# Strided attention heads: from one fused VectorE instruction per query row and key row to GpSimd products summed by VectorE

## The chip, the core and the metric

The program runs on one core of a Trainium2 chip. The metric is the device time of one execution in microseconds (us). A core has five engines that run side by side, each through its own queue in order: PE (TensorE, matrix products into PSUM), DVE (VectorE), ACT (ScalarE), POOL (GpSimd) and SP (SyncE, which issues the DMAs here). An instruction that waits for a semaphore holds everything behind it on its engine.

## The reference

Attention over 8 batches, 8 heads, 576 positions and 64 channels, followed by a feed-forward block on 4608 tokens of width 512 and inner width 2048, all in float32:

```python
scores = scale * np.matmul(q, k.transpose(0, 1, 3, 2))
mask_local = (rel >= 0) & (rel < stride)                     # stride = 32
mask_strided = (rel >= 0) & (pos[None, :] % stride == pos[:, None] % stride)
masks = np.stack([mask_local if h < H // 2 else mask_strided for h in range(H)], axis=0)
scores = np.where(masks[None, :, :, :], scores, -1000000000.0)
attn = softmax(scores)                                       # over the keys
x = attn @ v, as (tokens, heads * channels)
h = x @ w_in
out = (0.5 * h * (1.0 + erf(h * inv_sqrt2))) @ w_out
```

Heads 0 to 3 are local: a query sees the 32 positions up to its own. Heads 4 to 7 are strided: a query at position 32 r + p sees only positions 32 c + p with c up to r, that is at most 18 keys.

## The kernel before, in words

**Feed-forward.** The 4608 tokens are cut into 12 tiles of 384, the inner width into 16 blocks of 128, which makes 192 steps n. A step has an H product (`ffn_h`, L619 to L621: 12 matmuls of 384 columns), a Gelu in place on ACT (L628), a split of the result into a rounded high part `gh` (ACT, L630) and the remainder `gl` (DVE, L632), and an O product (`ffn_o`, L658 to L660: 9 matmuls of 512 columns, accumulated over the 16 blocks). The split, for weights and for the tokens `xh` and `xl` too, gives float32 precision out of TensorE's shorter format. H has two PSUM banks, so H of step n+2 may begin only when `gl` of step n has read the bank of step n. After the first 16 steps the program emits steps in pairs (`pair`, L867): H(n), H(n+1), O(n-2), O(n-1). The pools `gh` and `gl` have three buffers each.

**Local heads.** Their scores are matmuls (L297), their softmax is DVE and ACT work (L311, L315, L318 to L321), and their products with the values are matmuls (L337). In the main loop each token tile has a *visit*, once in 16 steps, in which PE does the value products of one tile and the scores of the next.

**Strided heads.** The 32 residues p times 4 heads make the 128 partitions. `sq`, `sk`, `sv` hold queries, keys and values as [128 partitions, 18 rows, 64 channels]. The first 12 rows of batch 0 are done by matmuls in the opening (L387 to L441). All other rows are cut into units of up to four query rows (`PLACE`, 37 units u from 3 to 39). For a unit, `strided_qk` (L480) takes the product of one query row with one key row by one DVE instruction that multiplies 64 channels and sums them (L494), 1290 times in all; each such instruction is followed in the profile by a read of the accumulator into `sc`. Then DVE takes the maximum and subtracts it (L502, L503), ACT takes the exponential (L504), DVE sums and divides (L520 to L524), and `strided_av` (L508) adds probability times value row to `acc`, one DVE instruction of 64 channels for each pair of rows (L534 for the first, L536 for the rest). DVE transposes `acc` into `xs` (L544); ACT and DVE split that into `xh` and `xl` (`to_x`, L235).

**What sets the order.** In the opening a list, `START`, sets the order of jobs on DVE, ACT, PE and SP: `c` splits the weights, `f` is a feed-forward step of the first tile, `u1` a part of the strided units of tile 1 (`unit_job`, L580). In the main loop (L889) only ACT and PE keep the program's order; DVE and POOL instructions are placed by the framework's scheduler. `run_strided` (L688) hands out the list `strided` in portions set by the costs that stand beside each operation (0.137 for a query-key product, 0.196 for a probability-value product, and so on), so that the work of a tile is spread over the steps before that tile is due. POOL's queue holds the masks and fills of the opening and one fill of `sc` for each unit (L487).

Of the kernel before, what the change touches and what calls it, by code (L numbers as in the profile page):

```python
# [10 lines left out]
F32 = mybir.dt.float32  # L11
# [50 lines left out]
HIGH_V = [0, 1, 2, 3, 5, 6, 10, 13]  # L62
QUOT_V = (0, 1)
ROWS = [(vi, b, r) for vi, (b, r0, r1) in enumerate(VISITS) for r in range(r0, r1)]


def units(most):
# [15 lines left out]
def attn_ffn_kernel(ctx: ExitStack, tc: tile.TileContext, qk, vl, qka, va, qs, ks, vs, w, out):  # L83
# [118 lines left out]
                lpool.tile([P, DM], F32, name=f"PT_{name}", tag="PT", bufs=2))  # L202

    def small(name):
        return [lpool.tile([P, 4], F32, name=f"{k}_{name}", tag=k, bufs=4) for k in ("nm", "ss", "rs")]

    def softmax_parts(blocks, nq, scores, msk, p, nmax, ssum, rs, dve):

# [271 lines left out]
    def strided_qk(u):  # L480
        vi, _, r0, nr, t, k = PLACE[u]
        W = r0 + nr
        ops = []

        def init():
            s = spool.tile([P, UR, NR], F32, name=f"sc_{u}", tag="sc", bufs=3)[:, 0:nr]
            nc.gpsimd.memset(s[:, :, 0:W], NEG)  # L487
            ss[u] = s
        ops.append((0.0, init))
        for c in range(W):  # L490
            for r in range(max(0, c - r0), nr):
                def f(r=r, c=c):
                    junk = spool.tile([P, D], F32, name=f"junk_{u}_{r}_{c}", tag="junk", bufs=4)
                    nc.vector.tensor_tensor_reduce(  # L494
                        junk, sq[vi, "q"][:, r0 + r, :], sq[vi, "k"][:, c, :], 1.0, 0.0,
                        ALU.mult, ALU.add, ss[u][:, r, c:c + 1])
                ops.append((0.137, f))

        def sm():
            s = ss[u][:, :, 0:W]  # L500
            m = spool.tile([P, UR], F32, name=f"m_{u}", tag="m")[:, 0:nr]
            nc.vector.tensor_reduce(m, s, AX.X, ALU.max)  # L502
            nc.vector.tensor_tensor(s, s, m.unsqueeze(2).to_broadcast([P, nr, W]), ALU.subtract)  # L503
            exps.append((u, lambda: nc.scalar.activation(s, s, AF.Exp, scale=SC)))  # L504
        ops.append((0.25, sm))
        return ops

    def strided_av(u):  # L508
# [13 lines left out]
        def quotients():  # L522
            s = ss[u][:, :, 0:W]
            nc.vector.tensor_tensor(s, s, every(z, W), ALU.mult)  # L524
            ss[u, "acc"] = spool.tile([P, UR, D], F32, name=f"acc_{u}", tag="acc", bufs=3)[:, 0:nr]
        ops += [(0.1, zsum), (0.1, lambda: nc.vector.tensor_scalar_add(z, z, 1e-9)),
                (0.1, lambda: nc.vector.reciprocal(z, z)), (0.1, quotients)]
        for c in range(W):
            for r in range(max(0, c - r0), nr):
                def f(r=r, c=c):  # L530
                    acc = ss[u, "acc"]
                    wgt = ss[u][:, r, c:c + 1]
                    if c == 0:
                        nc.vector.tensor_scalar_mul(acc[:, r, :], sq[vi, "v"][:, c, :], wgt)  # L534
                    else:
                        nc.vector.scalar_tensor_tensor(  # L536
                            acc[:, r, :], sq[vi, "v"][:, c, :], wgt, acc[:, r, :], ALU.mult, ALU.add)
                ops.append((0.196, f))

        def fin():  # L540
            acc = ss.pop((u, "acc"))
# [13 lines left out]
    def alternate(us, what, first):  # L555


        todo = []
        for u in us:
            ops = what(u)  # L560
            todo.append([[x] for x in ops[:first]] + [ops[first:-1]] + [[ops[-1]]])
        res = []
        for ops in zip(*todo):
            if len(ops[0]) == 1:
                res += [x[0] for x in ops]
                continue
            rows_ = []
            for u, x in zip(us, ops):
                r0, nr = PLACE[u][2:4]
                key = [r for c in range(r0 + nr) for r in range(max(0, c - r0), nr)]  # L570
                rows_ += [[f for k, f in zip(key, x) if k == r] for r in range(nr)]
            used = [-9] * len(rows_)
            while any(rows_):
                k = max((k for k in range(len(rows_)) if rows_[k]),
                        key=lambda k: (min(len(res) - used[k], 3), len(rows_[k])))
                used[k] = len(res)
                res.append(rows_[k].pop(0))
        return res

    def unit_job(us):  # L580

        n = 8
        qk = alternate(us, strided_qk, 1)
        for _, f in qk[:len(us)]:
            f()
        for i in range(len(us), len(qk), n):
            for _, f in qk[i:i + n]:
                f()
            yield
        for e in [x for x in exps if x[0] in us]:  # L590
# [1 line left out]
            e[1]()  # L592
        yield
        av = alternate(us, strided_av, 4)
        for i in range(0, len(av), n):
            for _, f in av[i:i + n]:
                f()
            yield
        todo = [x for x in splits if x[2] in us]
# [24 lines left out]
    def ffn_g(n):  # L624
        hp = hps.pop(n)
        gh = gpool.tile([P, TT], F32R, name=f"gh_{n}", tag="gh")
        gl = gpool.tile([P, TT], F32R, name=f"gl_{n}", tag="gl")
        nc.scalar.activation(hp, hp, AF.Gelu)  # L628
        yield
        nc.scalar.copy(gh, hp)  # L630
        yield
        nc.vector.tensor_tensor(gl, hp, gh.bitcast(F32), ALU.subtract)  # L632
        gs[n] = (gh, gl)
# [325 lines left out]
```

## Time and profile before

| What | us |
|---|---|
| time, median of 2 runs (875.14 to 876.11) | 875.62 |
| span of the profiled execution | 875.6 |
| PE busy | 853.6 |
| DVE busy | 707.1 |
| ACT busy | 490.3 |
| POOL busy | 17.6 |

The span of the profiled execution lies between the two timed runs, so that a sum made against it can be read as a time without a correction. The profile lists groups of instructions as line, engine, operation, output and inputs with their shapes and count, then busy time with the mean duration of one, then the idle time of the engine just before them and what ended it. Busy time of an engine counts overlapping instructions once; the busy time of a group adds up durations, so that groups of short DVE instructions, which overlap by a part of their length, add up to more than DVE's busy time.

### The profile page before, as it was taken

To read this page: it belongs to the slowest core of one execution; us is meant where nothing else is said; L and a number is where in the kernel's file an instruction comes from. 1 tells how busy PE (TensorE), PEld (TensorE's weight loads), DVE (VectorE), ACT (ScalarE), POOL (GpSimd) and SP (SyncE) were. 2 spreads that over 40 slices of the span, in tenths; PEclk is the share of its full clock that TensorE was granted. 3 is DMA by queue.
4 is the path that set the end of the run, shared out by engine and by line. 5 is a ranking of instruction groups with operands and counts; after the bars stand their busy time and mean duration, and the time that the engine had idled before them with its cause. 6 is when DMAs were issued, how large, how long until landed. Compare 5 with 4: busy or idle time off the path is not lost.

```text
span 875.6 us, 19724 instructions
## 1 busy us (share of the span) xinstructions
PE 853.6 (97%) x6082; PEld 768.4 (88%) x6082; DVE 707.1 (81%) x4901; ACT 490.3 (56%) x1005; POOL 17.6 (2%) x89
## 2 busy tenths in 40 slices
PE   6999999999999999999999999999999999999998
PEld 5787898899898989899889899999988988898997
DVE  6988999889989998998999879799898896751111
ACT  6978586466456274368366466546545735733222
POOL 5000100000000000000000000000000000000000
PEclk9799999999999999999999999999999999999999
DMA  9695211320310221310302221131032011000001
GB/s 350 226 372 207 96 42 24 123 76 7 128 45 19 93 75 33 98 49 8 110 28 67 67 67 43 34 123 46 8 101 79 9 34 44 32 8 6 31 1 37
DMA packets 34553, 66.68 MB, mean 76 GB/s; under 512 B 6800, under 2 KB 16528, under 8 KB 34448
## 3 DMA queue, kind: packets, MB, share of 16 engines
q1 hardware_dynamic: 34448, 65.43, 22.0%
q8 instruction: 48, 0.79, 0.4%
q14 instruction: 57, 0.47, 0.2%
HBM read 51.64 MB, written 9.44 MB: 70 GB/s over the span
## 4 chain that ended last, share of the span: by engine, by line
PE 69%; DVE 17%; DMA 5%; ACT 5%; issue 2%; SPq 2%; DVEq 0%; ACTq 0%
PE H L619 11%; PE O L659 11%; PE O L660 11%; PE H L621 11%; PE O L658 11%; PE H L620 11%; DVE acc L536 5%; DVE junk L494 4%; DMA ws<-in_w_dram 3%; DVE gl L632 2%; ACT L504 1%; SPq L326 1%; PE X_L L337 1%; ACT PT_L L315 1%; DVE xl L238 1%
## 5 line engine op out<-in xcount | busy, mean ns | idle before, releaser
L619 PE MATMUL H<-xh,w 128*128 128x384 f32 x768 | 260.8, 340 | 5.6 <-DVE gl L632 5.4
L620 PE MATMUL H<-xl,w 128*128 128x384 f32 x768 | 258.6, 337 | 0.8 <-DVE xl L238 0.8
L621 PE MATMUL H<-xh,w 128*128 128x384 f32 x768 | 258.9, 337 | 0.0
L628 ACT ACTIVATE H<-H 128x384 f32<-128x384 f32 x192 | 91.4, 476 | 287.4 <-PE H L621 230.5
L536 DVE SCALAR_TENSOR_TENSOR acc<-sv,sc,acc 128x64 f32<-128x64 f32 x1158 | 248.8, 277 | 0.6
L660 PE MATMUL O<-w,gl 128*128 128x512 f32 x576 | 226.8, 394 | 0.1
L659 PE MATMUL O<-w,gh 128*128 128x512 f32 x576 | 226.2, 393 | 0.0
L658 PE MATMUL O<-w,gh 128*128 128x512 f32 x576 | 225.0, 391 | 0.5 <-ACT gh L630 0.5
L494 DVE CUSTOM_DVE_ANT_0 junk<-sq,sk 128x64 f32<-128x64 f32 x1290 | 204.5, 217 | 3.3 <-DMA sk<-in_ks_dram 3.1
L632 DVE TENSOR_TENSOR gl<-H,gh 128x384 fp32r<-128x384 f32 x192 | 105.9, 551 | 105.8 <-ACT gh L630 105.7
L619 PEld LDWEIGHTS H<-xh,w 128*128 128x128 f32 x768 | 144.9, 189 | 12.7 <-DVE gl L632 7.5
L620 PEld LDWEIGHTS H<-xl,w 128*128 128x128 f32 x768 | 144.9, 189 | 4.8 <-DVE xl L238 1.2
L621 PEld LDWEIGHTS H<-xh,w 128*128 128x128 f32 x768 | 144.9, 189 | 0.1
L630 ACT CAST gh<-H 128x384 fp32r<-128x384 f32 x192 | 92.3, 481 | 69.2 <-PE O L659 62.8
L660 PEld LDWEIGHTS O<-w,gl 128*128 128x128 f32 x576 | 108.3, 188 | 24.4 <-DVE gl L632 1.6
L658 PEld LDWEIGHTS O<-w,gh 128*128 128x128 f32 x576 | 108.5, 188 | 21.1 <-ACT gh L630 1.0
L659 PEld LDWEIGHTS O<-w,gh 128*128 128x128 f32 x576 | 108.4, 188 | 20.6
L494 DVE DVE_READ_ACCUMULATOR2_ANT sc<- 128x1 f32 x1290 | 103.7, 80 | 0.0
L628 ACT ACT_TABLE_LOAD x62 | 79.5, 1283 | 1.1
L504 ACT ACT_TABLE_LOAD x35 | 44.9, 1283 | 0.6
L315 ACT ACTIVATE PT_L<-P_L,nm_L 128x64 f32<-128x64 f32 x132 | 44.3, 339 | 0.3
L315 ACT ACT_TABLE_LOAD x26 | 33.4, 1283 | 0.5
(114 smaller groups left out, 493.0 us busy)
## 6 DMA issues: line engine op xcount, KB each, us to landing
ws<-in_w_dram SPq DMA_DIRECT2D x16, 1023.8 KB, 9.9
qk<-in_qk_dram SPq DMA_DIRECT2D x36, 320.0 KB, 5.1
out_dram<-ob SPq DMA_DIRECT2D x34, 256.0 KB, 2.1
vl<-in_vl_dram SPq DMA_DIRECT2D x36, 192.0 KB, 3.9
sk<-in_ks_dram SPq DMA_DIRECT2D x8, 576.0 KB, 4.7
sv<-in_vs_dram SPq DMA_DIRECT2D x8, 576.0 KB, 4.0
band<-PT_L SPq DMA_DIRECT2D x240, 16.0 KB, 1.8
sq<-in_qs_dram SPq DMA_DIRECT2D x4, 576.0 KB, 4.8
```

The source lines that it names most:

```text
L315: nc.scalar.activation(pv[:, :, h, :], p1[:, h * 2 * QB:(h + 1) * 2 * QB].rearrange("p (c t) -> p c t", c=2), AF.Exp, bias=nm[:, h:h + 1], ...
L494: nc.vector.tensor_tensor_reduce(junk, sq[vi, "q"][:, r0 + r, :], sq[vi, "k"][:, c, :], 1.0, 0.0, ALU.mult, ALU.add, ss[u][:, r, c:c + 1])
L536: nc.vector.scalar_tensor_tensor(acc[:, r, :], sq[vi, "v"][:, c, :], wgt, acc[:, r, :], ALU.mult, ALU.add)
L619: nc.tensor.matmul(hp, w1[f][:, 0, c, :], xh[:, c, :], start=(c == 0), stop=False)
L620: nc.tensor.matmul(hp, w1[f][:, 0, c, :], xl[:, c, :], start=False, stop=False)
L621: nc.tensor.matmul(hp, w1[f][:, 1, c, :], xh[:, c, :], start=False, stop=(c == NC - 1))
L628: nc.scalar.activation(hp, hp, AF.Gelu)
L630: nc.scalar.copy(gh, hp)
L632: nc.vector.tensor_tensor(gl, hp, gh.bitcast(F32), ALU.subtract)
L658: nc.tensor.matmul(o, gh[:, sl], w2[f][:, 0, :], start=(f == 0), stop=False)
L659: nc.tensor.matmul(o, gh[:, sl], w2[f][:, 1, :], start=False, stop=False)
L660: nc.tensor.matmul(o, gl[:, sl], w2[f][:, 0, :], start=False, stop=(f == NF - 1))
```

## The change

The 1290 query-key instructions and the 1290 probability-value instructions are replaced. For one query row, GpSimd multiplies the row with up to nine key rows at once (up to 576 elements in a partition) into a buffer, and one VectorE reduction sums each run of 64 channels into `sc`. For the values GpSimd multiplies the value rows, read with the channel outside and the key row inside (a step of 64 elements), with the probabilities of the query row, and VectorE sums over the key rows into `acc`. Longer rows are cut into equal pieces. The buffers are two (`NPROD`), so that a product is emitted ahead of the sum of the piece before it. The products carry no cost in the list `strided`, the sums carry 0.15 + elements / 960. `small` has three buffers in place of four, `acc` two in place of three, and `gl` two in place of three. `alternate` no longer interleaves the rows of the units; `unit_job` yields five portions for queries and keys and six for the values.

```diff
+PRODUCT = 576
+NPROD = 2
+def MULT(nc):
+    return nc.gpsimd
+def cuts(n, most):
+    k = -(-n // most)
+    at = [i * n // k for i in range(k + 1)]
+    return list(zip(at, at[1:]))
+def staged(pieces, size, product, sums):
+    ops, late = [], []
+    for x in pieces:
+        c = 0.15 + size(*x) / 960
+        ops.append((0.0 * c, lambda x=x: product(*x)))
+        late.append((c, lambda x=x: sums(*x)))
+        if len(late) == NPROD:
+            ops.append(late.pop(0))
+    return ops + late
...
-        return [lpool.tile([P, 4], F32, name=f"{k}_{name}", tag=k, bufs=4) for k in ("nm", "ss", "rs")]
+        return [lpool.tile([P, 4], F32, name=f"{k}_{name}", tag=k, bufs=3) for k in ("nm", "ss", "rs")]
...
-                    nc.vector.tensor_tensor_reduce(
-                        junk, sq[vi, "q"][:, r0 + r, :], sq[vi, "k"][:, c, :], 1.0, 0.0,
-                        ALU.mult, ALU.add, ss[u][:, r, c:c + 1])
-                ops.append((0.137, f))
+        def product(r, lo, hi):
+            n = hi - lo
+            prods[r, lo] = pr = spool.tile([P, PRODUCT], F32, name=f"pq_{u}_{r}_{lo}", tag="prod", bufs=NPROD)[
+                :, 0:n * D].rearrange("p (c d) -> p c d", c=n)
+            MULT(nc).tensor_tensor(pr, sq[vi, "q"][:, r0 + r, :].unsqueeze(1).to_broadcast([P, n, D]),
+                                   sq[vi, "k"][:, lo:hi, :], ALU.mult)
+        def sums(r, lo, hi):
+            nc.vector.tensor_reduce(ss[u][:, r, lo:hi], prods.pop((r, lo)), AX.X, ALU.add)
...
-            ss[u, "acc"] = spool.tile([P, UR, D], F32, name=f"acc_{u}", tag="acc", bufs=3)[:, 0:nr]
+            ss[u, "acc"] = spool.tile([P, UR, D], F32, name=f"acc_{u}", tag="acc", bufs=2)[:, 0:nr]
...
-                        nc.vector.tensor_scalar_mul(acc[:, r, :], sq[vi, "v"][:, c, :], wgt)
-                    else:
-                        nc.vector.scalar_tensor_tensor(
-                            acc[:, r, :], sq[vi, "v"][:, c, :], wgt, acc[:, r, :], ALU.mult, ALU.add)
-                ops.append((0.196, f))
+        def product(r, lo, hi):
+            n, w_ = hi - lo, r0 + r + 1
+            prods[r, lo] = pr = spool.tile([P, PRODUCT], F32, name=f"pv_{u}_{r}_{lo}", tag="prod", bufs=NPROD)[
+                :, 0:n * w_].rearrange("p (d c) -> p d c", d=n)
+            MULT(nc).tensor_tensor(pr, sq[vi, "v"][:, 0:w_, lo:hi].rearrange("p c d -> p d c"),
+                                   ss[u][:, r, 0:w_].unsqueeze(1).to_broadcast([P, n, w_]), ALU.mult)
+        def sums(r, lo, hi):
+            nc.vector.tensor_reduce(ss[u, "acc"][:, r, lo:hi], prods.pop((r, lo)), AX.X, ALU.add)
...
-        gl = gpool.tile([P, TT], F32R, name=f"gl_{n}", tag="gl")
+        gl = gpool.tile([P, TT], F32R, name=f"gl_{n}", tag="gl", bufs=2)
```

DVE's queue in the main loop, before, from the remainder `gl` of step 64 on (the number behind a name is its step, unit or row; `ISA` is the fused product and sum, with the read of its accumulator behind it):

```order
L632 TENSOR_TENSOR gl_64_4806<-H_64_4792,gh_64_4805 128x384
L238 TENSOR_TENSOR xl_5_4811<-xs_16_4682,xh_5_4810 128x2x128
L536 SCALAR_TENSOR_TENSOR acc_17_4847<-sv_6_4416,sc_17_4418,acc_17_4847 128x64
L544 STREAM_TRANSPOSE xs_17_4951<-acc_17_4847 128x256
L494 ISA junk_20_0_0_5330,sc_20_5328<-sq_6_4012,sk_6_4014 128x64
L494 ISA sc_20_5328 128x1
L494 ISA junk_20_1_0_5332,sc_20_5328<-sq_6_4012,sk_6_4014 128x64
L494 ISA sc_20_5328 128x1
```

And now, from the same step to the remainder of the step behind it and a little further:

```order
L654 TENSOR_TENSOR gl_64_3976<-H_64_3962,gh_64_3975 128x384
L265 TENSOR_TENSOR xl_5_4021<-xs_16_3982,xh_5_4020 128x2x128
L527 TENSOR_REDUCE sc_19_4179<-pq_19_0_6_4183 128x7
L527 TENSOR_REDUCE sc_19_4179<-pq_19_1_0_4186 128x7
L654 TENSOR_TENSOR gl_65_4007<-H_65_3993,gh_65_4006 128x384
L527 TENSOR_REDUCE sc_19_4179<-pq_19_1_7_4227 128x7
L527 TENSOR_REDUCE sc_19_4179<-pq_19_2_0_4230 128x7
L527 TENSOR_REDUCE sc_19_4179<-pq_19_2_7_4264 128x8
```

Sums now stand between the remainders in place of fused products; each sum needs a GpSimd product (`pq`, `pv`), and `gl` stands behind it in the same queue.

The fullest kind of stretch on DVE lies ahead of the first `gl` of a pair with a visit. Now, the stretch ahead of `gl` of step 60 (behind these rows stand two more `xl` and eight score instructions of the local heads with their reads, and then `gl` of step 60):

```order
L654 TENSOR_TENSOR gl_59_3665<-H_59_3651,gh_59_3664 128x384
L580 STREAM_TRANSPOSE xs_16_3982<-acc_16_3942 128x256
L527 TENSOR_REDUCE sc_18_3984<-pq_18_0_0_3986 128x9
L527 TENSOR_REDUCE sc_18_3984<-pq_18_1_0_3988 128x5
L527 TENSOR_REDUCE sc_18_3984<-pq_18_1_5_3991 128x5
L527 TENSOR_REDUCE sc_18_3984<-pq_18_2_0_4034 128x5
L527 TENSOR_REDUCE sc_18_3984<-pq_18_2_5_4037 128x6
L527 TENSOR_REDUCE sc_18_3984<-pq_18_3_0_4040 128x6
L527 TENSOR_REDUCE sc_18_3984<-pq_18_3_6_4083 128x6
L535 TENSOR_REDUCE m_18_4087<-sc_18_3984 128x4
L536 TENSOR_TENSOR sc_18_3984<-sc_18_3984,m_18_4087 128x4x12
L265 TENSOR_TENSOR xl_4_3331<-X_L12_3697,xh_4_3330 128x2x128 x2
```

Seven sums stand in one row there; the remainder behind them is not reached before the seventh product.

POOL's queue in the main loop, before, one fill of `sc` for each unit (here units 16 to 20):

```order
L487 MEMSET sc_16_4168 128x4x4
L487 MEMSET sc_17_4418 128x4x8
L487 MEMSET sc_18_4684 128x4x12
L487 MEMSET sc_19_4953 128x4x16
L487 MEMSET sc_20_5328 128x36
```

And now, around the query-key products of unit 18:

```order
L567 TENSOR_TENSOR pv_16_3_0_3951<-sv_6_3810,sc_16_3556 128x256
L523 TENSOR_TENSOR pq_18_0_0_3986<-sq_6_3423,sk_6_3425 128x576
L514 MEMSET sc_19_4179 128x4x16
L523 TENSOR_TENSOR pq_18_1_0_3988<-sq_6_3423,sk_6_3425 128x320
L523 TENSOR_TENSOR pq_18_1_5_3991<-sq_6_3423,sk_6_3425 128x320
L523 TENSOR_TENSOR pq_18_2_0_4034<-sq_6_3423,sk_6_3425 128x320
L523 TENSOR_TENSOR pq_18_2_5_4037<-sq_6_3423,sk_6_3425 128x384
L523 TENSOR_TENSOR pq_18_3_0_4040<-sq_6_3423,sk_6_3425 128x384
L523 TENSOR_TENSOR pq_18_3_6_4083<-sq_6_3423,sk_6_3425 128x384
L567 TENSOR_TENSOR pv_17_0_0_4095<-sv_6_3810,sc_17_3812 128x320
```

All products stand in one queue, those of the keys of a unit ahead of those of the values of the unit before it. In the whole program there are now 402 products on POOL and 402 sums on DVE, 201 of each kind for queries and keys and for the values; the products have 82,560 elements in a partition for each kind, 165,120 together, 411 on average.

More of the change, by code (lines that the diff above doesn't have):

```diff
@@ L489, in strided_qk @@
         ops.append((0.0, init))
[L490 to L494, printed above, removed]
-                        junk, sq[vi, "q"][:, r0 + r, :], sq[vi, "k"][:, c, :], 1.0, 0.0,
-                        ALU.mult, ALU.add, ss[u][:, r, c:c + 1])
-                ops.append((0.137, f))
+        prods = {}
+        def product(r, lo, hi):
[6 more added lines that the diff above has]
+            nc.vector.tensor_reduce(ss[u][:, r, lo:hi], prods.pop((r, lo)), AX.X, ALU.add)
+        ops += staged([(r, lo, hi) for r in range(nr) for lo, hi in cuts(r0 + r + 1, PRODUCT // D)],
+                      lambda r, lo, hi: (hi - lo) * D, product, sums)
         def sm():
@@ L524, in quotients @@
             nc.vector.tensor_tensor(s, s, every(z, W), ALU.mult)
-            ss[u, "acc"] = spool.tile([P, UR, D], F32, name=f"acc_{u}", tag="acc", bufs=3)[:, 0:nr]
+            ss[u, "acc"] = spool.tile([P, UR, D], F32, name=f"acc_{u}", tag="acc", bufs=2)[:, 0:nr]
         ops += [(0.1, zsum), (0.1, lambda: nc.vector.tensor_scalar_add(z, z, 1e-9)),
                 (0.1, lambda: nc.vector.reciprocal(z, z)), (0.1, quotients)]
[L528 to L533, printed above, removed]
-                        nc.vector.tensor_scalar_mul(acc[:, r, :], sq[vi, "v"][:, c, :], wgt)
-                    else:
-                        nc.vector.scalar_tensor_tensor(
-                            acc[:, r, :], sq[vi, "v"][:, c, :], wgt, acc[:, r, :], ALU.mult, ALU.add)
-                ops.append((0.196, f))
+        prods = {}
+        def product(r, lo, hi):
[6 more added lines that the diff above has]
+            nc.vector.tensor_reduce(ss[u, "acc"][:, r, lo:hi], prods.pop((r, lo)), AX.X, ALU.add)
+        ops += staged([(r, lo, hi) for r in range(nr) for lo, hi in cuts(D, PRODUCT // (r0 + r + 1))],
+                      lambda r, lo, hi: (hi - lo) * (r0 + r + 1), product, sums)
         def fin():
@@ L559, in alternate, with pieces @@
         for u in us:
[L560 to L578, printed above, removed]
+            todo.append(what(u))
+        return [ops[0] for ops in todo] + [x for ops in todo for x in ops[1:]]
     def unit_job(us):
-        n = 8
+        def pieces(ops, n):
+            for i in range(n):
+                yield ops[i * len(ops) // n:(i + 1) * len(ops) // n]
         qk = alternate(us, strided_qk, 1)
@@ L585, in unit_job @@
             f()
-        for i in range(len(us), len(qk), n):
-            for _, f in qk[i:i + n]:
+        for part_ in pieces(qk[len(us):], 5):
+            for _, f in part_:
                 f()
@@ L594, in unit_job @@
         av = alternate(us, strided_av, 4)
-        for i in range(0, len(av), n):
-            for _, f in av[i:i + n]:
+        for part_ in pieces(av, 6):
+            for _, f in part_:
                 f()
```

## The prediction

> **What bounds the kernel now.** I read the page's engine rows first, then the busy time by stretches, then who waits for whom, and at last the chain of waits.
>
> ```profile
> PE 853.6 (97%) x6082; PEld 768.4 (88%) x6082; DVE 707.1 (81%) x4901; ACT 490.3 (56%) x1005; POOL 17.6 (2%) x89
> PE   6999999999999999999999999999999999999998
> DVE  6988999889989998998999879799898896751111
> PEclk9799999999999999999999999999999999999999
> ```
>
> ```profile
> 0.00:22.00 22.00, 13.36 (x434) 11.23 (x434) 13.41 (x60) 15.14 (x44) 11.17 (x54) 0.98 0.93 351
> ...
> 131.00:153.00 22.00, 20.49 (x139) 18.22 (x139) 21.78 (x174) 13.80 (x29) 0.11 (x1) 1.00 0.09 21
> 153.00:175.00 22.00, 20.33 (x203) 18.35 (x200) 19.70 (x134) 9.01 (x23) 0.11 (x1) 1.00 0.36 125
> ...
> 200.00:300.00 100.00, 100.00 (x767) 90.63 (x766) 94.68 (x777) 54.86 (x117) 0.84 (x6) 1.00 0.20 64
> ...
> 850.00:875.60 25.60, 21.67 (x107) 18.98 (x105) 2.23 (x4) 5.59 (x11) 0.00 (x0) 0.98 0.10 31
> ```
>
> The columns are the stretch, its length, busy time of PE, PEld, DVE, ACT and POOL, the granted clock, the DMA share and GB/s. PE is busy 853.6 of 875.6, at a clock of 1.00 in the steady part, and stands still 22.0 in all. Of that 8.6 (22.00 less 13.36) lie in the first 22 us and 3.9 (25.60 less 21.67) in the last stretch, which the change doesn't touch. Busy PE could still be PE waiting inside, so I look at the matmuls:
>
> ```profile
> 87.44 0.39 PE L658 MATMUL O<-w,gh 128*128 128x512 f32 x1
> 89.52 0.33 PE L619 MATMUL H<-xh,w 128*128 128x384 f32 x1
> 91.62 0.39 PE L658 MATMUL O<-w,gh 128*128 128x512 f32 x1
> ```
>
> An O product takes 2.08 (87.44 to 89.52), an H product 2.10, already before the strided work is at its full rate. The chain of waits gives the same pace for the main loop:
>
> ```profile
> 223.01 1.08 PE X_L L337 x32
> 224.56 1.10 PE S L297 x71
> 292.47 1.08 PE X_L L337 x32
> ```
>
> Visits are 69.46 apart; less the visit's own 2.18, eight pairs take 67.28, 8.41 each, against 8.36 for two H and two O. So PE is the bound, and DVE, though 95% busy, is only a near second. PE's own waits that this change could reach (total, times, longest):
>
> ```profile
> PE H L619 <- DVE gl L632: 5.4, 4, 2.1
> ...
> PE S L337 <- DMA band<-PT_L: 1.5, 1, 1.5
> ```
>
> **Part 1: what leaves DVE.**
>
> ```profile
> L536 DVE SCALAR_TENSOR_TENSOR acc<-sv,sc,acc 128x64 f32<-128x64 f32 x1158 | 248.8, 277 | 0.6
> L494 DVE CUSTOM_DVE_ANT_0 junk<-sq,sk 128x64 f32<-128x64 f32 x1290 | 204.5, 217 | 3.3 <-DMA sk<-in_ks_dram 3.1
> 243.73 3.57 DVE L536 SCALAR_TENSOR_TENSOR acc<-sv,sc,acc 128x64 f32<-128x64 f32 x18
> 292.78 0.22 DVE L494 CUSTOM_DVE_ANT_0 junk<-sq,sk 128x64 f32<-128x64 f32 x1
> 292.93 0.22 DVE L494 CUSTOM_DVE_ANT_0 junk<-sq,sk 128x64 f32<-128x64 f32 x1
> ```
>
> Instructions overlap: 18 value steps take 3.57, 0.198 each and not 0.277; a fused product with its accumulator read takes 0.15 (292.78 to 292.93). 1290 x 0.198 + 1290 x 0.15 = 449 leave DVE's queue. What comes is 402 sums over 165,120 elements. The nearest rows are reductions:
>
> ```profile
> L398 DVE TENSOR_REDUCE Am<-va 128x8 f32<-128x192 f32 x2 | 0.7, 352 | 0.0
> L520 DVE TENSOR_REDUCE z<-sc 128x4 f32<-128x16 f32 x7 | 1.0, 164 | 2.7 <-ACT sc L504 2.7
> ```
>
> (352 - 164) / 176 = 1.07 ns for an element and 0.147 fixed: 402 x 0.147 + 165,120 x 0.00107 = 236. DVE falls from 707 to about 494. That by itself is worth no more than what DVE now costs PE: 5.4 in four waits, in stretches such as 153 to 175 (DVE 19.70 of 22). With DVE a third emptier, but sums that wait for products in the same queue, I take a gain of 3, with 0 and 5.4 as bounds.
>
> **Part 2: the products on POOL.** The trace shows no product of two tensors on POOL; the nearest rows are a fill and a copy.
>
> ```profile
> L814 POOL MEMSET band<- 128x2048 f32 x1 | 1.8, 1813 | 2.6 <-DVE w L169 2.6
> L746 POOL MEMSET first<- 128x512 f32 x3 | 1.5, 530 | 0.1
> L726 POOL COPY mask<-mask 128x64 f32<-128x64 f32 x1 | 0.2, 238 | 0.1
> L729 POOL MEMSET bmask<- 128x64 f32 x2 | 0.3, 147 | 0.0
> ```
>
> One stream written costs (1813 - 530) / 1536 = 0.835 ns an element and 0.10 fixed. Low bound: both reads hide behind the write, 0.835. High bound: each read costs what the copy adds to the fill, (238 - 147) / 64 = 1.4, so 0.8 + 2 x 1.4 = 3.6. Between them three streams of 0.835 make 2.5, which I take, since the long fill is the better measured row. All products: 402 x 0.1 + 165,120 x 0.0025 = 453, against 178 and 635 at the bounds; the first two fit well, the third barely, into the some 700 between slice 4 of DVE's row and slice 36, where it drops (21.9 each). The total isn't what decides, the order is: DVE's queue is fixed, and where it puts sums that POOL hasn't fed, `gl` stands behind them and PE behind `gl`. In the main loop 374 sums with 160,640 elements stand in 79 pairs of steps. At 2.5, ten pairs ask more of POOL than the pair lasts (8.4, or 10.6 with a visit), by 5.9 in all; but two products can be ready ahead while DVE waits, about 2.2 of work, and with that carried over it is 0. At 3.0 it is 38 without and 9 with the carry, at 3.6 it is 106 and 58, at 0.835 nothing.
>
> The Trainium skill, GPSIMD Engine Reference, § 3.1, measures an add of two 2048-element tensors at 4497 ns, and § 7 says reads that step by more than 8 bytes cost half as much again; an estimate from them is 2.2 ns for the keys, 3.3 for the values, whose rows are read in steps of 64 elements. The sum by that page would be 402 x 0.1 + 82,560 x (2.2 + 3.3) / 1000 = 494 on POOL, with 2.5 to 23.5 in overfull pairs; their middle, 13, in place of my 4 gives a time 9 above mine. No run here shows it yet.
>
> The fullest stretch, worked out at 2.5: ahead of `gl` of step 60 stand sums of 576, 320, 320, 320, 384, 384 and 384 elements. A transpose of `acc` comes first (0.44). Two products are ready. The first sum (0.76) frees a buffer, five products follow (0.90, 0.90, 1.06 three times: 4.98), then the last sum (0.56): 6.7. Then `m` and its subtraction, four `xl`, eight score instructions, priced like the fused product at 0.15:
>
> ```profile
> L544 DVE STREAM_TRANSPOSE xs<-acc 128x256 f32<-128x256 f32 x29 | 12.6, 439 | 0.5
> L502 DVE TENSOR_REDUCE m<-sc 128x4 f32<-128x48 f32 x5 | 1.0, 196 | 0.0
> L238 DVE TENSOR_TENSOR xl<-X_L,xh 128x256 fp32r<-128x256 f32 x23 | 8.7, 416 | 0.0
> L238 DVE TENSOR_TENSOR xl<-S,xh 128x128 fp32r<-128x128 f32 x20 | 5.6, 282 | 0.0
> L632 DVE TENSOR_TENSOR gl<-H,gh 128x384 fp32r<-128x384 f32 x192 | 105.9, 551 | 105.8 <-ACT gh L630 105.7
> ```
>
> 0.4 + 2 x 0.416 + 2 x 0.282 + 8 x 0.15 = 3.0, and `gl` 0.55: 10.3. `gl` of step 59 may end 1.55 ahead of the pair's H(60) (part 3: the visit's 2.18 less 0.63), `gl` of step 60 is due when O(59) ends, 8.36 later: 9.9 long. So 0.4 late, on each of ten such visits: 4 in all. For the whole part the bounds are 0 and, at 3.0, about 24 (the middle of 9 and 38); what the hand-over of a buffer between the two engines costs the trace doesn't show, and it lies within them.
>
> **Part 3: two buffers for `gl`.** `gl` of step n must wait until O(n-2) has read its buffer. PE does H(n), H(n+1), O(n-2), O(n-1), H(n+2), and H(n+2) needs `gl` of step n. From the end of O(n-2) to H(n+2) is O(n-1), 2.08; `gl` takes 0.55. It costs nothing where DVE is there within the remaining 1.5; between `gl` of the first and second step of a pair stand at most three sums, two of them ready (two of about 0.6). The rows of `gl` show DVE now idle 105.7 ahead of it for `gh`, so a waiting `gl` with work queued behind it is no new thing. If the cover goes, each late `gl` moves PE by as much; that is counted in part 2. `acc` and `small` hold up nothing that is due within a step: 0.
>
> **Sum.** 875.6 - 3 + 4 = 876.6, so **877**. The profiled span is the time here; the median is 875.62.
>
> **Rivals.** *DVE had no spare time, and now it has* (15%): all 5.4 come back, nothing is late: 870. For: `gl` is the only DVE wait of PE. Against: nearly all of PE's time is matmul. *POOL is slower than the fills* (18%): between 2.5 and 3.0 nothing much, from about 3.0 on the overfull pairs add up; 900 at 3.0 (875.6 + 24), at 3.6 875.6 + 58 to 106, 934 to 982. For: the copy's 1.4; the strided reads. Against: the copy is a single short row. *The engines share a way into SBUF* (10%): DVE instructions with two SBUF inputs wait for a running product. These are
>
> ```profile
> L320 DVE TENSOR_TENSOR PT_L<-PT_L,rs_L 128x256 f32<-128x256 f32 x33 | 13.9, 421 | 1.2 <-DVE rs_L L319 0.6 <-DVE acc L536 0.2
> L238 DVE TENSOR_TENSOR xl<-xs,xh 128x256 fp32r<-128x256 f32 x29 | 12.1, 416 | 0.0
> ```
>
> with 8 smaller `xl` and 74 small ones on `sc`, 144. Half a product (0.56) each, with POOL at work 453 of 700, is 0.36 x 144 = 52; if half falls where `gl` has no room, 26: 902. It decides once the extra wait in a pair exceeds the 1.5 of part 3. The Trainium skill, SBUF — State Buffer, § Who interferes with whom, says just this: an instruction of VectorE with two SBUF inputs and a GpSimd instruction that reads SBUF exclude each other for their whole length, while a reduction never contends. With POOL at 17.6 busy the trace can't show it. That the change might not empty DVE, each sum waiting for its product, is within the forecast, whose gain is 3 of 5.4 for that reason.
>
> **How the numbers follow.** Forecast 877: 57%; 870: 15%; slow POOL: 18%, a third of it below 893; shared way: 10%, split about that line. The range goes from 868 (875.6 less all 5.4 and the 1.5 of PE's wait for `band`) to 902 (the ends of the slow cases at 3.0 and of the shared way); above it lies a POOL of over 3.0. Two per cent is 17.5, about what a measurement of this kernel can tell from no change. Faster than 858 would need 17.5 of the 22.0 that PE stands still, 12.5 of which are untouched: 2%. Slower than 893: two thirds of 18, half of 10 and a few of the forecast's own: 23%. Within: 75%.
>
> **What would show it.** In the profile after: DVE near 494 busy with long waits of `sc` and `acc` for POOL; products on POOL near 1.13 for 411 elements; PE's wait for `gl` under 10; visits 69.5 to 70 apart. Wrong, if visits lie over 71 apart, if a product of 512 elements takes over 1.65 (3.0 ns), or if small DVE instructions on `sc` take far over their 0.2.

## The result and the profile after

The changed kernel took 942.74 us (median of 2 runs, 939.88 to 945.59), 1.0765 times the kernel before, 95% interval 1.0686 to 1.0844. The forecast was 877, with 902 as the upper end. The profiled execution has a span of 937.9, 62.3 more than before. First the engine rows and slices of the page, as they were shown of before:

```profile
PE 881.3 (94%) x6082; PEld 777.8 (83%) x6082; DVE 534.5 (57%) x1433; ACT 481.8 (51%) x999; POOL 491.1 (52%) x491
PE   5999999999899999999989999989989998999998
DVE  5988686547655565646656655555756557351110
POOL 4023698337756465637947756744767577160000
```

DVE is emptier by 173 us, as meant, and POOL works half the time. PE is still the bound, but no longer without gaps: it stands still 937.9 less 881.3, 56.6, against 22.0 before, and its busy time has grown by 27.7 although it has the same 6082 matmuls. So there are two things to explain, gaps and slower matmuls. The waits (total, times, longest) name the gaps:

```profile
DVE gl L654 <- PE O L682: 124.2, 49, 5.8
DVE acc L571 <- POOL pv L567: 90.1, 121, 2.0
...
DVE z L553 <- ACT sc L537: 60.4, 29, 4.4
...
DVE sc L527 <- POOL pq L523: 41.7, 88, 1.1
...
PE H L641 <- DVE gl L654: 39.7, 33, 4.1
DVE ss_L L345 <- ACT PT_L L342: 36.8, 29, 5.8
```

H waits for `gl` 39.7 in place of 5.4: those 34.3 are the whole growth of PE's idle time (34.6). One engine further back `gl` itself waits 124.2 for O to release its buffer, a wait that does not stand in the list of before, while the 105.7 of waiting for `gh` are down to 3.4. Whatever else is queued on DVE stands behind that wait.

The longest of PE's gaps in the timeline (start, length, engine, line; in brackets the idle time before and what ended it), DVE first and then PE:

```profile
460.32 0.54 DVE L654 TENSOR_TENSOR gl<-H,gh 128x384 fp32r<-128x384 f32 x1
...
463.34 0.75 DVE L527 TENSOR_REDUCE sc<-pq 128x9 f32<-128x576 f32 x1 [0.64 <-POOL pq L523]
...
468.15 0.55 DVE L571 TENSOR_REDUCE acc<-pv 128x32 f32<-128x384 f32 x1 [0.70 <-POOL pv L567]
469.38 0.55 DVE L571 TENSOR_REDUCE acc<-pv 128x32 f32<-128x384 f32 x1 [0.67 <-POOL pv L567]
...
472.55 0.55 DVE L654 TENSOR_TENSOR gl<-H,gh 128x384 fp32r<-128x384 f32 x1
```

```profile
468.64 0.40 PE L682 MATMUL O<-w,gl 128*128 128x512 f32 x1
473.15 0.44 PE L641 MATMUL H<-xh,w 128*128 128x384 f32 x1 [4.12 <-DVE gl L654]
...
474.18 0.53 PE L643 MATMUL H<-xh,w 128*128 128x384 f32 x1
474.50 0.53 PE L641 MATMUL H<-xh,w 128*128 128x384 f32 x1
```

The second `gl` comes 12.2 after the first; O ended at 469, and PE stands 4.12. The wait of `gl` for O is not in this stretch: DVE stands five times for products of GpSimd, 3.1 in all, and works the rest of the time. The timeline shows the same for each of H's 33 waits, from the late `gl` back to the `gl` ahead of it: in 20 of them, 26.2 of the 39.7 us, DVE stood longest for products; in 12, 13.2 us, for ACT; in one it only worked.

Behind the gap something happens that no term of the prediction had: the matmuls start 0.32 apart, not 0.18. The stretches that follow (length, busy time of PE, PEld, DVE, ACT, POOL, then the granted clock) show why:

```profile
474.00:478.00 4.00, 4.00 (x16) 4.00 (x15) 2.66 (x6) 1.29 (x3) 4.00 (x6) 0.57 0.00 0
478.00:482.00 4.00, 4.00 (x20) 3.44 (x19) 1.57 (x12) 3.96 (x11) 1.70 (x2) 1.00 0.00 0
```

After the gap TensorE is granted 0.57 of its clock for some 4 us. The Trainium skill, TensorE: Matmul & The Clock Gate, Part 1, describes a monitor that halves the clock after an idle window of about 3.4 us and restores it after as long a busy one; the 4.12 gap and the 4 us at 0.57 agree. But four shorter gaps of this execution, of 2.09, 2.41, 3.02 and 3.06 us, were followed by a lower clock too, while those of 2.08 and 2.78 were not; here the measured gaps decide. Over the whole execution the mean granted clock falls from 0.992 to 0.982, which is 1% of 937.9, about 9 us on top of the gaps.

Visits, 69.46 apart before, now lie 76.7 apart (from one of them to the last, eight intervals):

```profile
229.99 1.15 PE L364 MATMUL X_L<-band,vl 96*64 96x64 f32 x32
...
843.59 1.15 PE L364 MATMUL X_L<-band,vl 96*64 96x64 f32 x32
```

### The profile page after: what moved, and what is told of

Its sections match the earlier page's. It is cut to its first block, busy times and chain, and to the rows that moved or that the text cites. A ratio compares the mean times of both kernels' runs of the same rounds, so it can differ in the third digit from the quotient of the medians.

```text
span 937.9 us, 16610 instructions
## 1 busy us (share of the span) xinstructions
PE 881.3 (94%) x6082; PEld 777.8 (83%) x6082; DVE 534.5 (57%) x1433; ACT 481.8 (51%) x999; POOL 491.1 (52%) x491
## 4 chain that ended last, share of the span: by engine, by line
PE 55%; DVE 12%; ACT 11%; POOL 10%; DMA 6%; issue 5%; SPq 0%; DVEq 0%; ACTq 0%; POOLq 0%
PE H L641 11%; PE H L643 10%; PE H L642 10%; PE O L681 8%; PE O L680 8%; PE O L682 7%; POOL pv L567 7%; DMA ws<-in_w_dram 3%; POOL pq L523 3%; ACT PT_L L342 3%; ACT L537 2%; ACT L342 2%; DVE PT_L L347 2%; DVE gl L654 2%; DVE ss_L L345 2%
## 5 line engine op out<-in xcount | busy, mean ns | idle before, releaser
L567 POOL TENSOR_TENSOR pv<-sv,sc 128x576 f32<-128x576 f32 (+12 forms) x201 | 262.8, 1337 | 278.2 <-DVE sc L557 243.7
L641 PE MATMUL H<-xh,w 128*128 128x384 f32 x768 | 270.3, 352 | 40.0 <-DVE gl L654 39.7
L643 PE MATMUL H<-xh,w 128*128 128x384 f32 x768 | 264.0, 344 | 1.2 <-DVE w L196 1.2
L642 PE MATMUL H<-xl,w 128*128 128x384 f32 x768 | 264.3, 344 | 0.0
L523 POOL TENSOR_TENSOR pq<-sq,sk 128x448 f32<-128x448 f32 (+8 forms) x201 | 215.2, 1095 | 70.7 <-DMA sk<-in_ks_dram 40.3
L680 PE MATMUL O<-w,gh 128*128 128x512 f32 x576 | 228.2, 396 | 0.0
L681 PE MATMUL O<-w,gh 128*128 128x512 f32 x576 | 228.0, 396 | 0.0
L641 PEld LDWEIGHTS H<-xh,w 128*128 128x128 f32 x768 | 147.4, 192 | 61.4 <-DVE gl L654 57.2
L654 DVE TENSOR_TENSOR gl<-H,gh 128x384 fp32r<-128x384 f32 x192 | 105.0, 547 | 127.8 <-PE O L682 124.2
L571 DVE TENSOR_REDUCE acc<-pv 128x32 f32<-128x448 f32 (+17 forms) x201 | 115.1, 575 | 90.8 <-POOL pv L567 90.1
L642 PEld LDWEIGHTS H<-xl,w 128*128 128x128 f32 x768 | 147.4, 192 | 2.7 <-DVE xl L265 0.4
L643 PEld LDWEIGHTS H<-xh,w 128*128 128x128 f32 x768 | 147.2, 192 | 1.5 <-DVE w L196 1.5
L527 DVE TENSOR_REDUCE sc<-pq 128x7 f32<-128x448 f32 (+8 forms) x201 | 114.8, 573 | 43.5 <-POOL pq L523 41.7
```

The lines of the kernel that those rows point to most:

```text
L523: MULT(nc).tensor_tensor(pr, sq[vi, "q"][:, r0 + r, :].unsqueeze(1).to_broadcast([P, n, D]), sq[vi, "k"][:, lo:hi, :], ALU.mult)
L527: nc.vector.tensor_reduce(ss[u][:, r, lo:hi], prods.pop((r, lo)), AX.X, ALU.add)
L567: MULT(nc).tensor_tensor(pr, sq[vi, "v"][:, 0:w_, lo:hi].rearrange("p c d -> p d c"), ss[u][:, r, 0:w_].unsqueeze(1).to_broadcast([P, n, w ...
L571: nc.vector.tensor_reduce(ss[u, "acc"][:, r, lo:hi], prods.pop((r, lo)), AX.X, ALU.add)
L641: nc.tensor.matmul(hp, w1[f][:, 0, c, :], xh[:, c, :], start=(c == 0), stop=False)
L642: nc.tensor.matmul(hp, w1[f][:, 0, c, :], xl[:, c, :], start=False, stop=False)
```

## The experiments

**Which part of the change costs the time.** The first four runs shared one chip with runs of the kernel before (876.99).

```diff
 kernel before
-        gl = gpool.tile([P, TT], F32R, name=f"gl_{n}", tag="gl")
+        gl = gpool.tile([P, TT], F32R, name=f"gl_{n}", tag="gl", bufs=2)
```

> The kernel before with one part of the change alone: two buffers for gl in place of three. Theory (the time is lost where sums and softmax steps wait on VectorE ahead of gl): 875 to 882, since VectorE waits for nobody there. Rival A (the two gl buffers alone make gl late): 900 or more, with PE waiting over 20 us for gl.

Measured: 927.44, ratio 1.0573 [1.0557, 1.0589]. The theory fails and rival A holds: two buffers of `gl` alone, with nothing on GpSimd, cost 50.4 us, of the 67.1 (942.74 less 875.62) that the whole change costs. The waits:

```profile
DVE gl L632 <- PE O L660: 81.2, 32, 5.8
...
DVE z L520 <- ACT sc L504: 57.5, 30, 4.6
DVE ss_L L318 <- ACT PT_L L315: 44.7, 23, 7.0
PE H L619 <- DVE gl L632: 39.6, 33, 3.7
```

H's wait for `gl` is 39.6 against 39.7 in the changed kernel, and the waits of `z` and `ss_L` for ACT are there too, so they come with the buffers and not with the products. Its mean granted clock is 0.982, as in the changed kernel. But waits are only half of what makes `gl` late here. The longest gap, DVE and then PE:

```profile
609.37 0.54 DVE L632 TENSOR_TENSOR gl<-H,gh 128x384 fp32r<-128x384 f32 x1
...
622.11 0.55 DVE L632 TENSOR_TENSOR gl<-H,gh 128x384 fp32r<-128x384 f32 x1
```

```profile
622.71 0.66 PE L619 MATMUL H<-xh,w 128*128 128x384 f32 x1 [3.73 <-DVE gl L632]
```

In these 12.7 us DVE never stands still: 57 fused products with their reads and the eight score instructions of the local heads lie between the two `gl`. Of the 33 waits of H, 10 with 19.8 of the 39.6 us are of this kind; in the other 23 DVE stood for ACT. One thing more comes with the buffer: the scheduler that places DVE's instructions makes another order for two buffers than for three. In the built programs, which list the queue of each engine and the address of each tile, the score instructions of a visit stand behind `gl` of step 60 in the kernel before, and ahead of it here. So 50.4 is the price of the buffer together with the order that the scheduler makes for it.

```diff
 def MULT(nc):
-    return nc.gpsimd
+    return nc.vector
```

> The whole change, but with the 402 products issued to VectorE in place of GpSimd. VectorE then does 165,120 elements more, about 200 us. Theory (waits for GpSimd and for ScalarE ahead of gl): the waits for products are gone, 875 to 890. Rival A (gl buffers): still 900 or more. Rival B (the two engines share a way into SBUF): also 875 to 890, since GpSimd is idle.

Measured: 965.64, ratio 1.1008 [1.0978, 1.1039]; H waits 54.7 for `gl`. Of the expectations only rival A's holds. More work on DVE makes it worse, so GpSimd's taking the products helps as long as `gl` is short of buffers.

```diff
-            nc.vector.tensor_reduce(ss[u][:, r, lo:hi], prods.pop((r, lo)), AX.X, ALU.add)
+            nc.vector.tensor_reduce(ss[u][:, r, lo:hi], sq[vi, "k"][:, lo:hi, :], AX.X, ALU.add)
...
 (and the sums for the values read sv in the same way)
```

> The whole change, with all products on GpSimd, but each sum reads the keys or values themselves in place of the product, so that no sum waits for GpSimd; the products are computed and read by nobody, so the strided half of the attention is left out of the result. Theory: 875 to 890. Rival B (shared way): instructions of VectorE are as long as in the changed kernel (0.56 for the scalar addition of ss_L, 0.68 for PT_L) and the time stays over 915. Rival A: 900 or more.

Measured: 983.1, ratio 1.1206 [1.118, 1.1232]. The theory fails; rivals A and B both allow this (`ss_L` takes 0.86 here and `PT_L` 0.79). The edit does not free the sums of GpSimd altogether: they still wait 34.0, 14 times, for the fills of `sc`, which stand behind the products in GpSimd's queue.

```diff
 as above, and
-            MULT(nc).tensor_tensor(pr, sq[vi, "q"][:, r0 + r, :].unsqueeze(1).to_broadcast([P, n, D]),
-                                   sq[vi, "k"][:, lo:hi, :], ALU.mult)
...
 (and the product for the values)
```

> As the run before, and the products on GpSimd left out as well (the strided half of the attention is left out of the result). Theory: as the run before or up to 5 us less. Rival B: at least 30 us less than the run before. Rival A: 900 or more here too, with gl waiting for PE's O product.

Measured: 962.65, ratio 1.0974 [1.0951, 1.0998], 20.5 less than the run before, between the theory and rival B; rival A holds. With no wait for products, and even with no product at all, the kernel is 20 to 40 us slower than the changed one. The rows of the run without products:

```profile
DVE gl L652 <- PE O L680: 211.8, 74, 5.9
DVE ss_L L345 <- ACT PT_L L342: 84.9, 27, 5.8
...
PE H L639 <- DVE gl L652: 52.9, 36, 3.9
```

A DVE that is done sooner reaches the next `gl` or `ss_L` sooner and stands there longer. What it gains is spent in the waits of its own queue. But the scheduler's order differs too: between `gl` of steps 59 and 60 the built programs have 30 instructions in the changed kernel, 37 and 22 in these two. So the two runs don't show what waiting for products costs in the changed kernel, and why `gl` comes even later in them stays open.

**Giving the buffer back.** Three buffers of `gl` don't fit beside two product buffers of 576 elements, so the pieces are cut to 384 first. The next four runs shared a chip (before: 876.84).

```diff
-PRODUCT = 576
+PRODUCT = 384
```

> The changed kernel with products of at most 384 elements in place of 576, still two buffers for gl: 548 products and sums in place of 402. It is the control for the next run. New theory (two gl buffers leave 1.5 us for every gl, and any wait ahead of it on VectorE is felt): 935 to 955, within 12 of the changed kernel. Rival (waits for single long products cost the time): below 925.

Measured: 927.37, ratio 1.0581 [1.0561, 1.0601]. H's wait for `gl` falls from 39.7 to 28.9, and the mean clock rises from 0.982 to 0.989 (0.7% of 925, 6 us); these two, 17 us, cover the 15 gained. Neither range holds: the time lies 8 below the theory's and 2 above the rival's. So with two buffers shorter products do bring something back; in 24.0 of H's 29 us of waiting here DVE stood longest for products.

```diff
-PRODUCT = 576
+PRODUCT = 384
...
-        gl = gpool.tile([P, TT], F32R, name=f"gl_{n}", tag="gl", bufs=2)
+        gl = gpool.tile([P, TT], F32R, name=f"gl_{n}", tag="gl")
```

> As the run before with gl's third buffer back (the shorter products make the room). New theory: 50 less than the run before, 880 to 900. Rival (waits for products and for the shared way cost the time, gl's buffers only where VectorE is full): less than 20 below the run before.

Measured: 890.38, ratio 1.0154 [1.0138, 1.0169]: 37 us less by one buffer, in the range expected, though 50 less were expected. `gl` itself waits for nothing but `gh` now, while DVE waits for GpSimd no less than before:

```profile
DVE gl L654 <- ACT gh L652: 132.3, 51, 5.5
DVE acc L571 <- POOL pv L567: 98.2, 167, 1.3
...
DVE sc L527 <- POOL pq L523: 46.4, 115, 1.1
...
PE H L641 <- DVE gl L654: 4.8, 7, 1.6
```

PE waits 4.8 for `gl`, so with three buffers these 145 us of waiting for products cost PE next to nothing.

```diff
 as above, and
-    with tc.manual_schedule(engines={ET.Activation, ET.PE}):
+    with tc.manual_schedule(engines={ET.Activation, ET.PE, ET.DVE}):
         for n in range(NB, NS, 2):
```

> As the run before, with VectorE in the main loop in the order of the program, as PE and ScalarE are, in place of the scheduler's order. If what is left over the kernel before comes from sums and softmax steps that the scheduler put ahead of gl: 5 to 15 less than the run before, 870 to 885. If it comes from the products' own pace: the same as the run before or slower.

Measured: 884.72, ratio 1.0095 [1.0076, 1.0113]: 5.7 less, as in the first case.

> As the run before the last (third gl buffer, scheduler's order), without products on GpSimd and with sums that read keys and values themselves; the strided half of the attention is left out of the result. New theory: 872 to 885, over 70 less than the same without the third buffer (962.65). Rival (an emptier VectorE runs into waits for ScalarE that stand ahead of gl, whatever the buffers): 900 or more.

Its edit is the pieces of 384, the third buffer of `gl`, and products and waits left out as above. Measured: 896.36, ratio 1.0221 [1.0206, 1.0237], between the theory and its rival; again no faster without the products. 8 to 20 us over the kernel before stayed in these three, at a granted clock of 0.99, though in the first two PE stood still no longer than before (23.8 and 18.1 against 22.0; in the third 29.2).

**The rest: slower matmuls at full clock.** The distance from the start of one matmul to the next of the same product, averaged between 200 and 780 us, tells more. H had 175.6 ns before and 177.5 in the run with 384 and three buffers; O had 229.1 and 234.1. All kernels so far with the change's code had O near 234, those without products too; the kernel before with two `gl` had 229.1. What was left was the place of the weights in SBUF: `small` has three tiles that take 32 bytes a partition each, and a buffer less of each puts the weight pool behind it 96 bytes lower, so weight tiles start at 32 past a multiple of 64 bytes, where they started on one (the first at 89888 in the built program of the changed kernel, at 88960 in that of the kernel before). Of what TensorE reads for H and O only the weights lie behind `small`. The next four shared a chip (before: 876.88).

```diff
 kernel before
-        return [lpool.tile([P, 4], F32, name=f"{k}_{name}", tag=k, bufs=4) for k in ("nm", "ss", "rs")]
+        return [lpool.tile([P, 4], F32, name=f"{k}_{name}", tag=k, bufs=3) for k in ("nm", "ss", "rs")]
```

> The kernel before with one number of the change alone: the small softmax tiles (nm, ss, rs) have 3 buffers instead of 4. Each such tile takes 32 bytes of a partition, so the pool that lies behind, that of the weights, starts 96 bytes lower: each weight tile starts 32 bytes past a multiple of 64 where it started on one. Theory place (TensorE reads weight tiles that start off a multiple of 64 bytes more slowly): the pitch of the O matmuls in the main loop (start to start, mean) goes from 229 to 234 ns and that of the H matmuls from 175.6 to about 177.5; 1728 O by 5 ns and 2304 H by 2 ns are 13 us: time 885 to 890. Rival: the longer pitch comes from something else in the changed code (its orders, its GpSimd products, its tiles): pitch 229 and time 875 to 878. Second rival: with 3 buffers a softmax step waits for the one before; then the time is longer but the pitch stays at 229.

Measured: 888.22, ratio 1.0129 [1.0104, 1.0154], O 234.0 and H 177.3 ns. The first matmuls of a pair's O and of the next pair's H in the timeline, before and then here:

```profile
381.06 0.33 PE L619 MATMUL H<-xh,w 128*128 128x384 f32 x1
385.25 0.39 PE L658 MATMUL O<-w,gh 128*128 128x512 f32 x1
389.37 0.33 PE L619 MATMUL H<-xh,w 128*128 128x384 f32 x1
```

```profile
381.40 0.39 PE L658 MATMUL O<-w,gh 128*128 128x512 f32 x1
385.60 0.34 PE L619 MATMUL H<-xh,w 128*128 128x384 f32 x1
389.84 0.40 PE L658 MATMUL O<-w,gh 128*128 128x512 f32 x1
```

18 O matmuls take 4.12 (385.25 to 389.37) before and 4.20 (381.40 to 385.60) here, 24 H matmuls 4.19 and 4.24: 0.13 for a pair of steps, 12 us for 96 pairs. The theory of the place holds.

```diff
 kernel before
-        return [lpool.tile([P, 4], F32, name=f"{k}_{name}", tag=k, bufs=4) for k in ("nm", "ss", "rs")]
+        return [lpool.tile([P, 4], F32, name=f"{k}_{name}", tag=k, bufs=5) for k in ("nm", "ss", "rs")]
```

> The kernel before with 5 buffers of the small softmax tiles instead of 4, which the change does not have: nothing can wait longer than before, but the weight tiles start 96 bytes higher, again 32 bytes past a multiple of 64. Theory place: as with 3 buffers, O pitch 234 ns and 885 to 890 us. Rival that 3 buffers make something wait: 875 to 878 here, pitch 229. Rival something else in the changed code: 875 to 878, pitch 229.

Measured: 883.36, ratio 1.0081 [1.0055, 1.0106], O 233.4 and H 175.9 ns. The time is a little below the range expected. A buffer more, which can make nothing wait, is slower too, and O by nearly as much: it is the place. H is slower only with three buffers; that part, 3 us (1.4 ns for each of 2304), is not explained.

> The run with products of at most 384 elements and three buffers of gl, with 4 buffers of the small softmax tiles again, so that the weight tiles start on a multiple of 64 bytes as before. It took 1.0154 of the kernel before with 3. Theory place: O pitch back at 229 ns, 10 to 13 us less: 877 to 881 us, 1.000 to 1.005. Rival, something else in the changed code: no change, 889 to 891 us.

The edit is pieces of 384 and three buffers of `gl`, with `bufs=4` in `small`. Measured: 879.88, ratio 1.0036 [1.0017, 1.0054], O 229.0 and H 175.8 ns: 10.5 us less than with three buffers of the small tiles, as the place predicts. H waits 9.5 for `gl`, 4.1 more than before, and PE's idle time is longer by 4.0 (26.0 against 22.0), about the 3.0 (879.88 less 876.88) that are left over the kernel before. In 10 of the 11 waits DVE only worked between the two `gl` and stood for no product.

> As the run before this one, with VectorE's instructions of the main loop in the order of the program instead of the scheduler's; with 3 buffers of the small tiles that took 1.0095. Theory place: pitch 229 ns, 871 to 875 us, 0.995 to 1.000, so level with or a little under the kernel before. Rival, something else in the changed code: 884 to 886 us.

The same with VectorE in the program's order. Measured: 872.71, ratio 0.9958 [0.9942, 0.9974], as expected. DVE waits 177 for products in it and H only 2.2 for `gl`.

**Whether the terms add up, and what the products bring.** The last three shared a chip (before: 875.81).

> The changed kernel with 4 buffers of the small softmax tiles again, so that its weight tiles start on a multiple of 64 bytes; gl keeps two buffers. Theory that the terms add up (two buffers of gl some 50, place of the weights 11, the rest a few us): 930 to 934 us, O pitch 229 ns. Rival, the slower reads are hidden in the waits for gl, since these take up whatever PE gives: 938 to 943 us although the pitch is 229.

The edit is `bufs=4` in `small` alone. Measured: 939.19, ratio 1.0722 [1.0687, 1.0756], O 229.1 ns. The rival held: PE's busy time falls by 8.5, and its idle time grows by as much, 6.0 of it in the row that was 39.7:

```profile
PE 872.8 (93%) x6082; PEld 773.9 (83%) x6082; DVE 536.2 (57%) x1433; ACT 481.5 (51%) x999; POOL 490.2 (52%) x491
```

```profile
PE H L641 <- DVE gl L654: 45.7, 35, 4.3
```

While `gl` is late, DVE and not PE sets the pace, and faster matmuls only wait longer. So the 11 us are the price of the place where PE is the bound; in the changed kernel they were hidden, for the 3.6 between the two medians are within the noise (1.0722 [1.0687, 1.0756] against 1.0765 [1.0686, 1.0844]). Of the 27.7 by which PE's busy time had grown, these 8.5 and the clock's 9 leave some 10 that no run takes apart.

> The changed kernel with VectorE's instructions of the main loop in the order of the program instead of the scheduler's; gl keeps two buffers and the small tiles three. Theory that the scheduler's order is what makes two buffers too few (it puts sums and softmax steps ahead of gl): PE's wait for gl falls from 40 us to under 15 and the time to 895 to 915 us. Rival, two buffers are too few in any order, since gl of step n can't begin before O(n-2) ends and VectorE holds back what is queued behind: 935 to 950 us.

The edit is the program's order on VectorE, in the changed kernel. Measured: 931.38, ratio 1.0618 [1.0576, 1.0659]; the time lies between the two ranges. H waits 34.1 for `gl`, and `gl` waits 212.9 for O. Two buffers are too few in this order too; the scheduler's order adds some 11 us. Here DVE stood for a product ahead of the late `gl` in all 33 waits of H, so with two buffers the products do hold PE up. The kernel before with two buffers in the program's order was not run.

> The kernel before with VectorE's instructions of the main loop in the order of the program. With the products on GpSimd, three buffers of gl and the weights in their old place that order took 0.9958 of the kernel before. Theory that this gain is the order's alone, and the products on GpSimd bring nothing: 870 to 874 us here too. Rival, the emptier VectorE is what lets that order gain: 876 us or more here.

The edit is the same in the kernel before. Measured: 869.48, ratio 0.9922 [0.9893, 0.9951], the lowest median of all and a little below the range expected. Its rows:

```profile
PE 849.1 (98%) x6082; PEld 767.5 (88%) x6082; DVE 722.8 (83%) x4901; ACT 490.6 (57%) x1005; POOL 17.5 (2%) x89
```

```profile
PE H L619 <- DVE gl L632: 1.4, 1, 1.4
```

The wait for `gl` goes by the order alone, with DVE at 722.8. Beside it the version with the products (0.9958) is no faster: an emptier DVE was worth nothing here.

## Why the prediction was wrong

**Part 3 failed, "two buffers for `gl`", priced at 0.** A run of the buffer alone costs 50.4. The slack of 1.5 was worked out rightly and then tested only against the sums between two `gl`. Two things were left out. First, the condition "where DVE is there" was taken from a kernel in which `gl` had a buffer more. With two buffers `gl` cannot begin before O has ended, DVE stands there (124.2 in all), what is queued behind comes late, and the next `gl` pays for whatever lies ahead of it beyond the 1.5. That is not one thing: without products it was waits for ACT (19.7 of 39.6 us) and plain work (19.8), in the changed kernel waits for products (26.2 of 39.7) and for ACT (13.2), in the program's order products in every wait. That the total is the same with and without products is measured; that the late start behind O lets all this through is read from the waits, and no run separates the buffer from the order that the scheduler makes for it in the kernel before. Second, the sentence "a waiting `gl` with work queued behind it is no new thing" compared 105.7 of waiting for `gh` with waiting for O. The first ended early enough that H waited 5.4 in all; the second ends one product, 2.08, ahead of the H that needs `gl`. "If the cover goes, each late `gl` moves PE by as much" was the right warning, but it was counted in part 2, for late sums alone. And a late `gl` costs more than its delay: PE's idle time grew by 34 in the run of the buffer alone, the clock fell by 0.010 of 925.8, 9 us more, and the remaining 7 of its 50 were not taken apart.

**In the same part, "`acc` and `small` hold up nothing: 0".** As waits that holds, but `small` moved the weights: 11.3 us by itself where PE is the bound, nothing clear of the noise in the changed kernel. The prediction had no term for a place in memory. `acc` was not run alone; in the version that is 1.0036 it has its two buffers.

**Part 2 was about right on the price of a product, not on what late sums cost.** Two lengths of each kind, with the mean in ns ahead of the idle time:

```profile
L523 POOL TENSOR_TENSOR pq<-sq,sk 128x576 f32<-128x576 f32 x31 | 44.1, 1442 | 5.0 <-DVE sc L527 4.3 <-DVE acc L571 0.8
L567 POOL TENSOR_TENSOR pv<-sv,sc 128x576 f32<-128x576 f32 x23 | 40.7, 1786 | 47.7 <-DVE sc L557 46.2 <-DVE acc L571 1.4
L523 POOL TENSOR_TENSOR pq<-sq,sk 128x320 f32<-128x320 f32 x28 | 24.7, 890 | 4.6 <-DVE acc L571 2.3 <-DVE sc L527 1.5 <-DVE rs_L L346 0.8
L567 POOL TENSOR_TENSOR pv<-sv,sc 128x320 f32<-128x320 f32 x21 | 22.5, 1087 | 32.0 <-DVE sc L557 22.8 <-issue 9.2
```

From 320 to 576 elements that is 2.2 ns an element for keys and 2.7 for values, with 0.2 fixed, 478 us in all (215.2 + 262.8) against 453. By the estimate from the GPSIMD Engine Reference of the Trainium skill it was to be 2.2 and 3.3: its § 3.1 agrees; its § 7 gives strided reads a surcharge of a half, where 2.7 over 2.2 is a quarter. The stretch worked out, ahead of `gl` of step 60, took 9.7 from `gl` to `gl` where 10.3 was foreseen, and PE did not stand there. But it was not the fullest: at five other visits the like stretch took 10.9 to 12.9, with 2.6 to 4.9 of waiting, mostly for value products, and PE stood 14.7 in these five alone, where 4 in all had been foreseen. With three buffers and the place set right 3.0 remain, near the 4, but that is luck: in 10 of the 11 waits of that run no product was waited for.

**Part 1: no gain.** DVE fell to 534, not 494. The price of the sums is not the difference (229.9 in the groups of the page, 236 foreseen). The run without products has as many instructions on DVE; its engine row:

```profile
PE 885.8 (92%) x6082; PEld 781.5 (81%) x6082; DVE 482.3 (50%) x1433; ACT 482.0 (50%) x999; POOL 17.5 (2%) x89
```

With the products 52 us come on top. Some 14 of them lie with the sums, which take as long each (573 ns for the keys, 572 without products) but no longer run one into the next. The other 38 lie in instructions that got longer, the rival of the shared way; first a row of before, then the rows now:

```profile
L318 DVE TENSOR_SCALAR ss_L<-ss_L 128x4 f32<-128x4 f32 x33 | 5.5, 166 | 11.1 <-ACT PT_L L315 10.7
```

```profile
L347 DVE TENSOR_TENSOR PT_L<-PT_L,rs_L 128x256 f32<-128x256 f32 x33 | 22.6, 684 | 2.5 <-DVE rs_L L346 1.9 <-DVE sc L536 0.2
L265 DVE TENSOR_TENSOR xl<-xs,xh 128x256 fp32r<-128x256 f32 x29 | 19.0, 657 | 4.4 <-ACT xh L263 4.4
...
L345 DVE TENSOR_SCALAR ss_L<-ss_L 128x4 f32<-128x4 f32 x33 | 18.4, 559 | 36.8 <-ACT PT_L L342 36.8
...
L265 DVE TENSOR_TENSOR xl<-X_L,xh 128x256 fp32r<-128x256 f32 x23 | 8.7, 415 | 9.5 <-ACT xh L263 9.5
```

684 against 421, 657 against 416; the last row, of the same shape with one input from PSUM, is unchanged at 415. The Trainium skill, SBUF — State Buffer, § Who interferes with whom, says this of two SBUF inputs, and the trace agrees. But `ss_L` has one tensor as input and went from 166 to 559, a third of the 38 us: two inputs are not the whole of it. So this rival was true as a mechanism. Its price in the changed kernel was not measured: leaving the products out where no sum waits for them brought 20.5 with two buffers, but these contain the waits for the fills of `sc`. With three buffers no price is seen (890.38 with products, 896.36 without). And the 3 us of gain had their place in the scheduler's order, not in DVE's load: that order alone brought H's wait down to 1.4 with DVE as full as before.

**The tests set beforehand.** Products near their price, DVE's waits for POOL: right. DVE near 494: wrong. "PE's wait for `gl` under 10" and "visits 69.5 to 70 apart": wrong at once, and they pointed at `gl`. The slower side was given a chance of 0.23, most of it for a POOL slower than the fills and for the shared way; two buffers of `gl` had no chance of their own, and they cost the most.

## What to carry to other kernels

A buffer that looks spare is also the lead of an in-order engine over its consumer: before taking one away, compare the slack that is left (1.5 here) with all that can stand ahead on that engine, its longest wait (5.8) and its longest stretch of work (12.7), and price a late hand-over above its own length. Where a scheduler places the instructions, look also at the order that it makes for the new count. Where tile sizes or buffer counts change, look at what moves behind them in memory, and measure the distance between matmuls. And emptying an engine brings nothing as long as the order of its queue, and not its load, makes the bound wait.

## What the runs showed of the hardware that was not expected

Weight tiles that start 32 bytes past a multiple of 64 make the O matmuls of 512 columns 2% slower (233.4 to 234.1 ns, at starts of 88864, 89056 and 89888 bytes in the built programs, against 229 at 88960 and 89984), at the same granted clock of 0.99. For H, whose stationary operand these tiles are, 175.6 went to 177.3 in one such place and to 175.9 in another.
